# VectorE makes both low parts of an expert's weight block

## The chip, the cores and the metric

The kernel runs on one core of one Trainium2 chip. The metric is the device time of one execution in microseconds (us). A core has TensorE (PE; its weight loads are shown as PEld), VectorE (DVE), ScalarE (ACT), GpSimd (POOL) and SyncE (SP, which here issues most of the DMAs). Each engine runs its own queue in order and waits for the others by semaphores.

## The reference

Attention with pooled keys and values, a token mixer, a channel mixer, and a mixture of eight experts, all in float32:

```python
# attention: 8 batches, 8 heads, 576 tokens, head size 64; keys and values pooled by 8
scores = scale * np.matmul(q, k_p.transpose(0, 1, 3, 2))
attn = softmax(scores);  x = attn @ v_p                  # 8 x 576 x 512
# token mixing, then channel mixing
h = np.maximum(x.transpose(0, 2, 1) @ w_tok1, 0.0) @ w_tok2
u = x + h.transpose(0, 2, 1)
x = u + np.maximum(u @ w_ch1, 0.0) @ w_ch2               # w_ch1 512 x 1536
# experts: each token goes to one of 8
logits = x @ w_gate;  local_gate = sigmoid(x @ w_local)
e = argmax(logits[b, s]) if s == 0 or local_gate[b, s] < 0.5 else prev_e
out[b, s] = p[e] * (np.maximum(x[b, s] @ w1[e], 0.0) @ w2[e])   # w1[e] 512 x 1024, w2[e] 1024 x 512
```

## The kernel before

A matrix in float32 is multiplied as two parts that TensorE takes at full rate: a high part (the value rounded by a cast to float32r) and a low part (the value less its high part). A product is three passes: high by high, low weights by high, high weights by low.

There are three stages. The mixer (attention and token mixing) runs to about 310 us. The channel mixer then works on 18 *slots* of 256 tokens with 6 blocks of 256 hidden features each, to about 936 us. The expert stage works on slots of the tokens of one expert: doubles of 256 tokens, four blocks each, with a single of 128 tokens after every third double in its later part. A step of the pipeline is one block of one slot (`pipeline`): `hidden` (L626; L642 for a single) makes relu(x @ w1 block) in PSUM, ScalarE casts its high part hh (L632) and VectorE its low part hl (L633); `project` (L668), one step later, adds hidden @ w2 block to y. At a slot's last step TensorE transposes the next slot's rows, ScalarE casts their high part xh (L616) and VectorE makes the low part xl (L617). Between the products VectorE computes the router's logits, 18 operations named junk for each 256 tokens of the channel stage (L697), and the tables of the experts' slots.

The weights come in blocks of w1[:, 256 features] and w2[256 features, :], 1 MB in float32. `load_expert` has SyncE load a block into one of four staging buffers st (L579, L583). `split_block` (L589) makes its four parts in a ring of six buffers w: two casts by ScalarE (L593, L595) and two subtractions, the low part of w1 (L594) and that of w2 (L596). With `aside`, for the first two blocks, which are split during the mixer, all four are GpSimd's.

The order on each engine is the order in which this code is written. In a step: the hidden's matmuls, the gathers of coming slots' rows (first step of a slot), the transposes (last step), some of the queued routing work (`drain`), the projects of the step before, and then `stage_to` and `split_to`: the load of the block eight ahead of the one just projected and the split of the block six ahead, whose ring buffer has become free. A cast therefore stands on ScalarE before the next step's hh, and a subtraction on VectorE before the next step's hl.

GpSimd has other work in the same queue: the scatter of each token's entry into the list of its expert (L791, four for each 512 tokens, each waiting for the one before to land), the gather of a slot's rows (L950) and the scatter of its output (L977).

Of the kernel before, what the change touches and what calls it, by code (L numbers as in the profile page):

```python
# [10 lines left out]
F32 = mybir.dt.float32  # L11
# [15 lines left out]
DCH = 1536  # L27
E, FE = 8, 1024

# Attention: 128-row chunks of a batch's (head, pooled key) rows, and the heads that each one meets.  # L30
NCH = 5
CH_ROWS = [128, 128, 128, 128, 64]
CH_HEAD0 = [0, 1, 3, 5, 6]
CH_NH = [2, 3, 3, 3, 2]
NT = 5

# Matrix blocks of 256 hidden features: w1[:, block] and w2[block, :] side by side.
FC = 256
NCC = DCH // FC
NCE = FE // FC  # L40
RING = 6

# Routed tokens: an expert's entries lie in a region of RS entries; DUM is where empty ones lie.
SLOT = 256
NSLOT = NTOK // SLOT
NGROUP = NSLOT // 2
# [5 lines left out]
FIRST_SINGLE = 7  # L52
EVERY = 3
NLATE = NDBL + NSGL
# The slots in the order in which they run: singles between the doubles, and those that may be empty last.
MAYBE = NSLOT + NSTATIC


# [5 lines left out]
RS = NTOK + SLOT  # L64
DUM = E * RS
LR = DUM + SLOT
# The greatest float32 z for which 1 / (1 + exp(-z)) rounds to 0.5 or more lies above this.
GATE = -1.5 * 2.0**-23


# [35 lines left out]


class PoolStack:
    """Tile pools at one end of the memories, released last first."""

    def __init__(self, tc, side):
        self.tc, self.side, self.pools = tc, side, []
# [9 lines left out]


class Slot:
    """A run of up to 256 tokens with the tiles that they are in."""


class Rounding:
    """float64 (as int64 words) rounded to float32, in steps that other work can lie between."""

    def __init__(self, nc, pool, ebias, src):
        self.nc, self.src = nc, src
# [41 lines left out]


def mixer_phase(nc, tc, q, k, v, w_tok1, w_tok2, w_ch1, w_ch2, const, stage, ebias, wc, u, spread):
    """Attention and token mixing: rows of u; and the channel weights in float32."""
    ident, mask = const("ident"), const("mask")
    late, early = PoolStack(tc, "right"), PoolStack(tc, "left")
    wp = late.pool("tokw", 1)  # L180
# [51 lines left out]
    rounding = {}  # L232

    def tok_piece(i):
        """Rounding of the i-th piece of the token weights, and its split."""
        src, h, l = tok_parts[i]
        r = Rounding(nc, cvp, ebias, src)
        r.fields()
        r.scale_here()
        r.size()  # L240
        f = r.sign()
        nc.scalar.copy(h, f)
        nc.gpsimd.tensor_sub(l, f, h.bitcast(F32))
        if i == NT - 1:
            nc.scalar.copy(t1h[64:, i], f)

    def piece(c, part):
        """Part of the rounding of the c-th piece of the channel weights."""
        if not 0 <= c < 4 * NCC:
            return  # L250
        if part == "fields":
            rounding[c] = Rounding(nc, cvp, ebias, ch_st[c // 2][:, c % 2 * 512:c % 2 * 512 + 512])
            rounding[c].fields()
        elif part == "scale":
            rounding[c].scale()
        elif part == "size":
            rounding[c].size()
        else:
            o = c // 2 % 2 * 1024 + c % 2 * 512
            nc.sync.dma_start(out=wc[c // 4, :, o:o + 512], in_=rounding.pop(c).sign())  # L260
# [160 lines left out]
    def mix1(b, t):  # L421
        n = rows(t)
        if t == 0:
            bps[b] = [psb.tile([128, 512], F32, tag=f"b1{m}", name=f"b1{m}") for m in range(2)]
        ps = bps[b]
        xh, xl = xh_t.pop((b, t)), xl_t.pop((b, t))
        for m in range(2):
            ms = slice(m * 128, m * 128 + 128)
            h, l = t1h[:, t, ms], t1l[:n, t, ms]
            # Half a tile of tokens has its two parts one above the other.  # L430
            passes = ((h, xh), (l, xh), (h, xl)) if n == 128 else ((h, xh), (l, xh[:n]))
            for i, (w, x) in enumerate(passes):
                nc.tensor.matmul(
                    ps[m], w, x, start=t == 0 and i == 0, stop=t == NT - 1 and i == len(passes) - 1
                )
# [37 lines left out]
    for c in range(NCH):  # L473
        k_sums(0, c)
    k_blocks(0)
    # The pieces of the channel weights that the steps round: none in those that end a batch's first product.
    pieces = {}
    for n in range(8, NS):
        if n % NT != 1:
# [62 lines left out]


def tail_phase(nc, tc, const, stage, wring_a, wc, w1, w2, w_gl, ctok, cempty, u, x2d, lst, out):
    """Channel mixing, routing and experts, 256 tokens at a time: the part that runs early, and the rest."""
    P = Slot()

    ident, before, rev, region = (const(n) for n in ("ident", "before", "rev", "region"))
# [14 lines left out]
        for r in range(EARLY_GROUPS * 2 * SLOT, NTOK + 128, 128):  # L563
            nc.sync.dma_start(out=x2d[r:r + 128], in_=zero)

# [1 line left out]
    def ring_tile(pos):  # L567
        p = wring_a if pos < 2 else P.ring_b if pos < 4 else P.ring_c
        return p.tile([128, 4, 1024], F32R, tag=f"w{pos}", name=f"w{pos}")
# [17 lines left out]
        return st  # L587

    def split_block(st, pos, aside=False):  # L589
        """A block's parts; aside: by the one engine that has little else to do."""  # L590
        w = ring_tile(pos)
        copy = nc.gpsimd.tensor_copy if aside else nc.scalar.copy
        copy(w[:, 0], st[:, :1024])  # L593
        (nc.gpsimd if aside else nc.vector).tensor_sub(w[:, 1], st[:, :1024], w[:, 0].bitcast(F32))  # L594
        copy(w[:, 2], st[:, 1024:])  # L595
        nc.gpsimd.tensor_sub(w[:, 3], st[:, 1024:], w[:, 2].bitcast(F32))  # L596
        k1 = lambda i: w[:, i].rearrange("p (k f) -> p k f", f=FC)
        k2 = lambda i: w[:, i].rearrange("p (s d) -> p s d", d=DM)
        return k1(0), k1(1), k2(2), k2(3)

# [1 line left out]

    def transpose_rows(sl):
        n = sl.nt * 128
# [12 lines left out]
            nc.vector.tensor_sub(sl.xl[:, ks, :n], ps[:, :, :n], sl.xh[:, ks, :n].bitcast(F32))  # L617

    def hidden(sl, w):
        """relu(x @ w1 block), features on the partitions, in two float32r parts."""  # L620
        w1h, w1l, _, _ = w
        ps = P.psh.tile([128, 2, SLOT], F32, tag="h", name="h")
        passes = [(a, x, k) for a, x in ((w1h, sl.xh), (w1l, sl.xh), (w1h, sl.xl)) for k in range(4)]
        for s in range(2):
            for i, (a, x, k) in enumerate(passes):
                nc.tensor.matmul(  # L626
                    ps[:, s], a[:, k, s * 128:s * 128 + 128], x[:, k],
                    start=i == 0, stop=i == len(passes) - 1,
                )
        hh = P.hT.tile([128, 2, SLOT], F32R, tag="hh", name="hh")  # L630
        hl = P.hT.tile([128, 2, SLOT], F32R, tag="hl", name="hl")
        nc.scalar.activation(hh, ps, AF.Relu)  # L632
        nc.vector.scalar_tensor_tensor(hl, ps, 0.0, hh.bitcast(F32), op0=ALU.max, op1=ALU.subtract)  # L633
        return hh, hl

    def hidden_rows(sl, w):
        """relu(x @ w1 block), tokens on the partitions."""
        w1h, w1l, _, _ = w
        ps = P.psh.tile([128, 2, SLOT], F32, tag="h", name="h")
        passes = [(a, x, k) for a, x in ((w1h, sl.xh), (w1l, sl.xh), (w1h, sl.xl)) for k in range(4)]  # L640
        for i, (a, x, k) in enumerate(passes):
            nc.tensor.matmul(  # L642
                ps[:, 0], x[:, k, :128], a[:, k], start=i == 0, stop=i == len(passes) - 1
            )
        h = P.hT.tile([128, FC], F32, tag="hrow", name="hrow")
        nc.scalar.activation(h, ps[:, 0], AF.Relu)
        return h
# [22 lines left out]
                    start=j == 0 and i == 0, stop=j == sl.nb - 1 and i == len(passes) - 1,  # L670
                )

# [1 line left out]
    queue = deque()  # L674

    def drain(budget):
# [5 lines left out]
            fn()  # L682
            budget -= cost

# [1 line left out]
    state = {"carry": None, "base": None}  # L686
    logit_t = {}

# [113 lines left out]
        queue.append((0.0, sums))  # L802
        queue.append((2.0, place))

# [1 line left out]
    one_row = lambda shape, name: P.route1.tile([1, *shape], F32, name=name)  # L806

    def running(x, name):
# [2 lines left out]
        return y  # L811

    def lookup(cum, first, idx, n, name):
        """For each of n indices: its expert under the running sums, and first[expert]."""
        ge = one_row([n, E], name + "g")
        nc.vector.tensor_tensor(
            ge, cum.rearrange("p (o e) -> p o e", o=1).to_broadcast([1, n, E]),
# [13 lines left out]
        return ex, at  # L831

    def shifted(x, add, shift, name):
        """floor((x + add) / 2 ** shift)"""
        i = P.route1.tile([1, E], I32, name=name + "i")
        nc.vector.tensor_scalar(i, x, float(add), None, op0=ALU.add)
        nc.vector.tensor_scalar(i, i, shift, None, op0=ALU.logical_shift_right)
        y = one_row([E], name)
        nc.vector.tensor_copy(y, i)
        return y  # L840
# [76 lines left out]
        nc.vector.tensor_scalar(ap, ap, float(DUM), None, op0=ALU.add)  # L917
        tables["late"] = table(ep, ap, NLATE, "ltab")

# [1 line left out]
    slots = []  # L921
    for i in range(NSLOT):
        s = Slot()
# [55 lines left out]
                in_=o[:, t], in_offset=None,  # L979
            )  # L980

# [1 line left out]
    blocks = [("c", j) for j in range(NCC)]  # L983
    for s in slots[NSLOT:]:
        s.block = len(blocks)
# [28 lines left out]
    tokid = const("tok")  # L1014

    def ahead(n):
        """Between the steps of the mixer: the first weight blocks."""
        if n == B * NT - 6:
            stage_to(2)
        elif n in (B * NT - 4, B * NT - 2):  # L1020
            split_to(nsplit[0] + 1, aside=True)
            stage_to(nsplit[0] + 2)

    def pipeline(slots, nrows, begin=None):
        # A project follows its hidden by one step, or two where the hidden block is turned first.
        steps = [(s, j) for s in slots for j in range(s.nb)]
        turn, ready = None, []
        for n, (s, j) in enumerate(steps):
# [154 lines left out]
```

## Time and profile before

| what | value |
|---|---|
| time, three runs | 1473.81, 1474.2, 1477.3 us; median 1474.2 |
| profiled execution, span from first to last instruction | 1476.5 us (no other time is listed for it) |
| busy: PE, PEld | 1405.3 (95%), 1241.5 us (84%) |
| busy: DVE, ACT, POOL | 964.6 (65%), 541.9 (37%), 550.7 us (37%) |
| mean granted clock of TensorE | 0.983 |

A line of a timeline tells when an instruction began, how long it took, its engine and line, the tiles it writes and reads, and in brackets how long its engine was idle before it and what ended that. A wait is read by its right side: "PE h L626 <- DVE hl L633" is TensorE idle before a matmul of L626 until VectorE's hl was there. [...]

### The profile page before, as it was taken

How to read it: one execution, taken by the hardware profiler on the slowest of the kernel's cores; microseconds unless marked ns; L12 is line 12 of the kernel's file. 1: busy time of each engine (PE TensorE's matmuls, PEld its weight loads, DVE VectorE, ACT ScalarE, POOL GpSimd, SP SyncE). 2: the span in 40 equal slices, each digit the busy share in tenths (PEclk: the TensorE clock that was granted, in tenths of full speed). 3: DMA queues.
4: the chain of work that ended last, by engine and by line, in shares of the span. 5: the costliest groups of instructions: out<-in, count | busy, mean ns of one | idle time of the engine just before them, and what ended most of it. 6: DMA issues, size and time to landing. Idle time of an engine off the chain costs nothing. (4 is left out here: it accounts for less than half of the span.)

```text
span 1476.5 us, 23732 instructions
## 1 busy us (share of the span) xinstructions
PE 1405.3 (95%) x8724; PEld 1241.5 (84%) x8724; DVE 964.6 (65%) x1880; ACT 541.9 (37%) x1357; POOL 550.7 (37%) x521
## 2 busy tenths in 40 slices
PE   5899999999999999999999999999879899898997
PEld 4677787789999999999999999889769798787986
DVE  6899888854565565656565756886484656666552
ACT  4677777641111111111111112443434454444551
POOL 4787665330010101010000001654665665656652
PEclk9999999999999999999999999999999999999999
DMA  9567776563010111111211113653775757567550
GB/s 265 143 211 221 234 220 196 175 219 109 29 30 29 30 29 30 29 30 30 49 15 52 30 44 115 196 172 133 249 254 175 261 182 249 200 217 256 200 205 24
DMA packets 161530, 204.40 MB, mean 138 GB/s; under 512 B 59568, under 2 KB 104752, under 8 KB 160496
## 3 DMA queue, kind: packets, MB, share of 16 engines
q1 hardware_dynamic: 153856, 181.81, 39.8%
q0 software_dynamic: 7552, 21.02, 3.9%
q8 instruction: 71, 1.16, 0.4%
q14 instruction: 51, 0.42, 0.1%
HBM read 164.68 MB, written 38.36 MB: 138 GB/s over the span
## 5 line engine op out<-in xcount | busy, mean ns | idle before, releaser
L668 PE MATMUL y<-w,hh 128*128 128x512 f32 x1504 | 414.9, 398 | 7.0 <-ACT hh L632 7.0
L626 PE MATMUL h<-xh,w 128*128 128x256 f32 x2880 | 408.3, 285 | 13.7 <-DVE hl L633 13.7
L626 PEld LDWEIGHTS h<-xh,w 128*128 128x128 f32 x2880 | 386.8, 193 | 29.7 <-DVE hl L633 15.3
L632 ACT ACTIVATE hh<-h 128x512 fp32r<-128x512 f32 x180 | 107.6, 598 | 584.4 <-PE h L626 406.9
L668 PEld LDWEIGHTS y<-w,hh 128*128 128x128 f32 x1504 | 271.6, 190 | 55.2 <-ACT hh L632 7.5
L633 DVE SCALAR_TENSOR_TENSOR hl<-h,hh 128x512 fp32r<-128x512 f32 x180 | 124.0, 689 | 276.3 <-ACT hh L632 276.1
L596 POOL TENSOR_TENSOR w<-st,w 128x1024 fp32r<-128x1024 f32 x94 | 234.6, 2514 | 107.4 <-ACT w L595 102.1
L594 DVE TENSOR_TENSOR w<-st,w 128x1024 fp32r<-128x1024 f32 x92 | 191.4, 2081 | 104.6 <-ACT w L593 103.9
L626 PE MATMUL h<-xl,w 128*128 128x256 f32 x1440 | 236.1, 286 | 11.8 <-DVE xl L617 11.4
L697 DVE SCALAR_TENSOR_TENSOR junk<-x,gate 128x512 f32<-128x512 f32 x324 | 234.3, 723 | 9.2
L668 PE MATMUL y<-w,hl 128*128 128x512 f32 x752 | 233.8, 392 | 2.3 <-DVE hl L633 2.3
L791 POOL DMA_INDIRECT entries<-ent,posi x36 | 40.5, 1124 | 516.6 <-DVE posi L789 349.1
L626 PEld LDWEIGHTS h<-xl,w 128*128 128x128 f32 x1440 | 201.1, 194 | 14.0 <-DVE xl L617 13.8
L668 PEld LDWEIGHTS y<-w,hl 128*128 128x128 f32 x752 | 141.9, 189 | 34.2 <-DVE hl L633 2.7
L593 ACT CAST w<-st 128x1024 fp32r<-128x1024 f32 x92 | 96.4, 1048 | 172.5 <-PE y L668 81.5
L364 ACT ACTIVATE e<-qk,mx 128x72 f32<-128x72 f32 (+1 forms) x320 | 97.1, 327 | 13.3 <-DVE sm L375 12.9
L595 ACT CAST w<-st 128x1024 fp32r<-128x1024 f32 x92 | 96.0, 1044 | 2.9 <-DMA st<-in_w_dram 2.9
L977 POOL DMA_INDIRECT out_dram<-x,entry x40 | 48.8, 1221 | 113.5 <-ACT w L593 27.0
L398 PE MATMUL pv<-vblk,aT 128*128 128x192 f32 (+5 forms) x400 | 73.8, 323 | 4.0 <-ACT aT L389 2.0
L398 PEld LDWEIGHTS pv<-vblk,aT 128*128 128x128 f32 (+3 forms) x400 | 58.0, 180 | 21.8 <-issue 10.3
L950 POOL DMA_INDIRECT rows<-x_rows,entry x40 | 45.6, 1141 | 79.7 <-DVE x L959 52.6
L364 ACT ACTIVATION_READ_ACCUMULATOR e<-qk,mx 128x1 f32 (+1 forms) x320 | 68.7, 215 | 0.0
(195 smaller groups left out, 1451.1 us busy)
## 6 DMA issues: line engine op xcount, KB each, us to landing
st<-in_w_dram SPq DMA_DIRECT2D x176, 512.0 KB
chs<-in_w_ch_dram SPq DMA_DIRECT2D x12, 1024.0 KB
rows<-u_rows SPq DMA_DIRECT2D x18, 512.0 KB
x_rows<-x SPq DMA_DIRECT2D x18, 512.0 KB
qin<-in_q_dram SPq DMA_DIRECT2D x32, 256.0 KB
kin<-in_k_dram SPq DMA_DIRECT2D x32, 256.0 KB
vin<-in_v_dram SPq DMA_DIRECT2D x32, 256.0 KB
u_rows<-ut SPq DMA_DIRECT2D x32, 256.0 KB
```

Source lines behind the costliest of these rows:

```text
L364: nc.scalar.activation(e[:n, h], ps[:n, h // 4, h % 4 * SP:h % 4 * SP + SP], AF.Exp, scale=1.0 / 64.0, bias=mx[:n, h:h + 1], accum_out=sm[ ...
L398: nc.tensor.matmul(ps[:n, h0 * D:(h0 + nh) * D], aT[:r, c, :n], vb[b % 2][:r, c, :nh].rearrange("p h d -> p (h d)"), start=c == 0, stop=c ...
L593: copy(w[:, 0], st[:, :1024])
L594: (nc.gpsimd if aside else nc.vector).tensor_sub(w[:, 1], st[:, :1024], w[:, 0].bitcast(F32))
L595: copy(w[:, 2], st[:, 1024:])
L596: nc.gpsimd.tensor_sub(w[:, 3], st[:, 1024:], w[:, 2].bitcast(F32))
L626: nc.tensor.matmul(ps[:, s], a[:, k, s * 128:s * 128 + 128], x[:, k], start=i == 0, stop=i == len(passes) - 1,)
L632: nc.scalar.activation(hh, ps, AF.Relu)
L633: nc.vector.scalar_tensor_tensor(hl, ps, 0.0, hh.bitcast(F32), op0=ALU.max, op1=ALU.subtract)
L668: nc.tensor.matmul(sl.y[t], x[:, s, ts], b[:, s], start=j == 0 and i == 0, stop=j == sl.nb - 1 and i == len(passes) - 1,)
L697: nc.vector.scalar_tensor_tensor(junk, sl.x2[:, t], 1.0, P.gate[:, e], op0=ALU.mult, op1=ALU.mult, accum_out=lt[:, 2 * a + t, e:e + 1],)
L977: nc.gpsimd.indirect_dma_start(out=out, out_offset=bass.IndirectOffsetOnAxis(s.ent[:, t, 0:1], 0), in_=o[:, t], in_offset=None,)
```

## The change

In `split_block` the engine that subtracts is chosen once and makes both low parts: VectorE, or GpSimd in a block that is split aside. Before, the low part of w2 was GpSimd's in every block. The casts and the order of the code are as they were. The rest of the diff takes out comments and docstrings; lines below `split_block` have numbers greater by one.

```diff
     def split_block(st, pos, aside=False):
         w = ring_tile(pos)
         copy = nc.gpsimd.tensor_copy if aside else nc.scalar.copy
-        copy(w[:, 0], st[:, :1024])
-        (nc.gpsimd if aside else nc.vector).tensor_sub(w[:, 1], st[:, :1024], w[:, 0].bitcast(F32))
-        copy(w[:, 2], st[:, 1024:])
-        nc.gpsimd.tensor_sub(w[:, 3], st[:, 1024:], w[:, 2].bitcast(F32))
+        sub = (nc.gpsimd if aside else nc.vector).tensor_sub
+        for i in range(2):
+            half = st[:, i * 1024:i * 1024 + 1024]
+            copy(w[:, 2 * i], half)
+            sub(w[:, 2 * i + 1], half, w[:, 2 * i].bitcast(F32))
```

VectorE's queue where the channel stage passes into the experts' (w_10045 and w_10114 are ring buffers of experts' blocks, x_9812 holds rows of the last but one channel slot). Before:

```order
L697 SCALAR_TENSOR_TENSOR junk,logit<-x_9812,gate 128x512 x4
L594 TENSOR_TENSOR w_10045<-st,w_10045 128x1024
L633 SCALAR_TENSOR_TENSOR hl<-h,hh 128x512
L617 TENSOR_TENSOR xl<-x_10081,xh 128x512
L617 TENSOR_TENSOR xl<-x_10088,xh 128x512
L697 SCALAR_TENSOR_TENSOR junk,logit<-x_9812,gate 128x512 x2
L594 TENSOR_TENSOR w_10114<-st,w_10114 128x1024
```

and after:

```order
L698 SCALAR_TENSOR_TENSOR junk,logit<-x_9812,gate 128x512 x4
L597 TENSOR_TENSOR w_10045<-st,w_10045 128x1024 x2
L634 SCALAR_TENSOR_TENSOR hl<-h,hh 128x512
L618 TENSOR_TENSOR xl<-x_10081,xh 128x512
L618 TENSOR_TENSOR xl<-x_10088,xh 128x512
L698 SCALAR_TENSOR_TENSOR junk,logit<-x_9812,gate 128x512 x2
L597 TENSOR_TENSOR w_10114<-st,w_10114 128x1024 x2
```

Each subtraction has become two, ahead of the next hl; nothing else has moved.

GpSimd's queue in the same stretch, before:

```order
L791 DMA entries<-ent,posi 39168x2 x4
L596 TENSOR_TENSOR w_9868<-st,w_9868 128x1024
L596 TENSOR_TENSOR w_9922<-st,w_9922 128x1024
L596 TENSOR_TENSOR w_9988<-st,w_9988 128x1024
L596 TENSOR_TENSOR w_10045<-st,w_10045 128x1024
L596 TENSOR_TENSOR w_10114<-st,w_10114 128x1024
L950 DMA rows<-x_rows,entry 128x512 x4
```

and after:

```order
L792 DMA entries<-ent,posi 39168x2 x28
L951 DMA rows<-x_rows,entry 128x512 x2
L792 DMA entries<-ent,posi 39168x2 x4
L951 DMA rows<-x_rows,entry 128x512 x6
L978 DMA out_dram<-x_10461,entry 4736x512 x2
```

The subtractions between the scatters and the gathers are gone; the DMAs stand in the same order.

VectorE's queue before the first channel slot (x_3957 and x_3964 are its transposed rows, w_3950 the third channel block), before:

```order
L443 SCALAR_TENSOR_TENSOR hl<-b_3722,hh 128x512
L594 TENSOR_TENSOR w_3950<-st,w_3950 128x1024
L617 TENSOR_TENSOR xl<-x_3957,xh 128x512
L617 TENSOR_TENSOR xl<-x_3964,xh 128x512
L455 TENSOR_TENSOR ut<-b_3973,x 128x512
```

and after:

```order
L443 SCALAR_TENSOR_TENSOR hl<-b_3722,hh 128x512
L597 TENSOR_TENSOR w_3950<-st,w_3950 128x1024 x2
L618 TENSOR_TENSOR xl<-x_3957,xh 128x512
L618 TENSOR_TENSOR xl<-x_3964,xh 128x512
L455 TENSOR_TENSOR ut<-b_3973,x 128x512
```

Here the added subtraction has come ahead of xl.

## Rows read from the trace of the kernel before

**Rows 1.** Waits of PE, 860 us to the end: us in total, times, longest.
```profile
PE h L626 <- DVE hl L633: 13.7, 3, 5.6
PE h L626 <- DVE xl L617: 11.4, 4, 6.0
PE y L668 <- ACT hh L632: 7.0, 2, 6.2
...
PE y L668 <- DVE hl L633: 2.3, 1, 2.3
```

**Rows 2.** Timeline, 1080 to 1120 us: start, us, what [idle before].
```profile
1090.17 11.03 DVE L594 TENSOR_TENSOR w<-st,w 128x1024 fp32r<-128x1024 f32 x1 [2.55 <-ACT w L593]
...
1090.73 9.38 POOL L596 TENSOR_TENSOR w<-st,w 128x1024 fp32r<-128x1024 f32 x4
...
1101.12 0.68 DVE L633 SCALAR_TENSOR_TENSOR hl<-h,hh 128x512 fp32r<-128x512 f32 x1
...
1102.46 1.39 PE L626 MATMUL h<-xl,w 128*128 128x256 f32 x4 [6.03 <-DVE xl L617]
```

**Rows 3.** Lines L594 and L596: count, ns min/median/max; group, busy us, mean ns.
```profile
L594 DVE TENSOR_TENSOR w<-st,w x92: 1205/1226/11033, 307.5 to 1442.0; 128x1024 fp32r<-128x1024 f32 x92
...
L594 POOL TENSOR_TENSOR w<-st,w x2: 2380/2547/2714, 269.2 to 276.9; 128x1024 fp32r<-128x1024 f32 x2
...
L596 POOL TENSOR_TENSOR w<-st,w x94: 2329/2412/3422, 273.0 to 1443.1; 128x1024 fp32r<-128x1024 f32 x94
...
L594 DVE TENSOR_TENSOR w<-st,w 128x1024 fp32r<-128x1024 f32 x92 | 191.4, 2081 | 104.6 <-ACT w L593 103.9 <-issue 0.6
```

**Rows 4.** Windows: start:end, us, then busy us (instructions) PE PEld DVE ACT POOL, PEclk, DMA, GB/s.
```profile
940.00:950.00 10.00, 9.39 (x54) 8.75 (x55) 7.26 (x11) 2.64 (x4) 7.00 (x6) 0.83 0.37 107
...
1100.00:1110.00 10.00, 7.54 (x31) 6.77 (x32) 5.73 (x8) 0.70 (x2) 1.60 (x3) 0.66 0.74 254
...
1350.00:1370.00 20.00, 16.25 (x94) 14.81 (x94) 10.85 (x8) 7.47 (x10) 11.50 (x6) 0.83 0.73 250
```

**Rows 5.** Timeline, 1016 to 1062 us, the chain behind one wait.
```profile
1028.53 0.96 POOL L791 DMA_INDIRECT entries<-ent,posi  x1 [3.18 <-DMA entries<-ent,posi]
...
1029.52 7.04 POOL L596 TENSOR_TENSOR w<-st,w 128x1024 fp32r<-128x1024 f32 x3
...
1031.95 0.37 SPq L579 DMA_DIRECT2D st<-in_w_dram  x1
...
1037.42 1.04 ACT L593 CAST w<-st 128x1024 fp32r<-128x1024 f32 x1 [14.29 <-DMA st<-in_w_dram]
...
1040.84 2.08 PE L668 MATMUL y<-w,hh 128*128 128x512 f32 x4 [6.23 <-ACT hh L632]
```

**Rows 6.** Timeline of DVE, 895 to 1060 us, and a window of the same stretch.
```profile
911.08 0.69 DVE L633 SCALAR_TENSOR_TENSOR hl<-h,hh 128x512 fp32r<-128x512 f32 x1 [2.50 <-ACT hh L632]
...
914.50 1.22 DVE L594 TENSOR_TENSOR w<-st,w 128x1024 fp32r<-128x1024 f32 x1
916.70 0.69 DVE L633 SCALAR_TENSOR_TENSOR hl<-h,hh 128x512 fp32r<-128x512 f32 x1 [0.98 <-ACT hh L632]
...
960.54 3.42 DVE L594 TENSOR_TENSOR w<-st,w 128x1024 fp32r<-128x1024 f32 x1
...
967.14 2.79 DVE L697 SCALAR_TENSOR_TENSOR junk<-x,gate 128x512 f32<-128x512 f32 x1
...
950.00:980.00 30.00, 30.00 (x194) 27.26 (x193) 28.29 (x52) 11.91 (x15) 13.55 (x8) 1.00 0.66 219
```

**Rows 7.** Timeline, 1100 to 1120 us: an hl and the project that reads it.
```profile
1113.36 0.69 DVE L633 SCALAR_TENSOR_TENSOR hl<-h,hh 128x512 fp32r<-128x512 f32 x1 [1.16 <-ACT hh L632]
...
1119.08 0.62 PE L668 MATMUL y<-w,hl 128*128 128x512 f32 x2
```

**Rows 8.** Timeline, 296 to 345 us: the first slot's xl.
```profile
308.97 1.29 DVE L617 TENSOR_TENSOR xl<-x,xh 128x512 fp32r<-128x512 f32 x2 [0.20 <-ACT xh L616]
...
310.55 0.64 PE L626 MATMUL h<-xl,w 128*128 128x256 f32 x4
```

More of the change, by code (lines that the diff above doesn't have):

```diff
@@ L124 @@
 class Slot:
+    pass
 class Rounding:
```

## The prediction

> **What bounds the kernel now.** I read the span and the PE waits first, then the lines, then the timeline around the longest waits. TensorE is busy nearly without a break from the first slot on, so the span is the sum of its matmuls and of whatever makes it wait or run slowly. In the expert stage it stands still four ways [rows 1]: 13.7 us for hl (3 times), 11.4 us for xl (4 times), 7.0 us for hh (twice) and 2.3 us for hl in a project (once), 34.4 us in ten waits. [...] Time lost is one minus the clock, times the stretch: 10 x 0.17 + 2 x 10 x 0.34 + 3 x 20 x 0.17 = 18.7 us.
>
> What causes the waits is seen in one place [rows 2]. At 1090.17 VectorE begins a subtraction of a block (L594) and at 1090.73 GpSimd begins four of its own (L596) back to back, 9.38 us; VectorE's takes 11.03 us and ends 1.1 us after GpSimd's last. Behind it on VectorE stand hl (1101.12) and the next slot's xl, and TensorE waits 6.03 us for xl. The subtraction itself needs 1.226 us (median of 92), yet the longest is 11.033 and GpSimd's median is 2.412 [rows 3]. The other waits for VectorE have a long subtraction or a held logit operation, as in [rows 6], in front of them in the same way.
>
> [...]
>
> One wait has another road [rows 5]. GpSimd issues the scatters of list entries (L791), one per landing (the last at 1028.53, after 3.18 us of waiting), and only then its subtractions, three in a row. SyncE's next load needs the staging buffer that the first of them frees and goes out at 1031.95; ScalarE's cast waits 14.29 us for it, hh stands behind the cast, and TensorE waits 6.23 us. That is GpSimd again, by way of a buffer.
>
> **The change part by part.** *Removed from GpSimd:* the low part of w2 of 92 blocks, 2.41 us each [rows 3]. GpSimd isn't waited for directly at the end, so its own time is worth nothing; what counts is that nothing stands in its queue that can hold VectorE, and that it no longer frees a staging buffer late. Both roads to the waits go: 34.4 + 18.7 = 53.1 us. Idle and low clock overlap a little inside the stretches of [rows 4] (a clock that falls while TensorE still waits costs nothing), so I take 52. Scatters and gathers stay on GpSimd; they come earlier.
>
> The two blocks that are split ahead, during the mixer, stay on GpSimd altogether (its two low parts of w1 are the L594 rows of POOL [rows 3]): no gain or loss there.
>
> *Added to VectorE:* 92 subtractions of the same shape as L594, so 92 x 1.226 = 113 us of work. It also loses what L594 has over its median: mean 2081 against 1226 ns [rows 3], 92 x 0.855 = 79 us, so its sum grows by only some 34 us. What matters is the fullest stretch. While the last logits are computed a step of VectorE is: hl and four logit operations, 911.08 to 914.50 = 3.42 us, then the subtraction [rows 6]; with two it is 3.42 + 2 x 1.226 = 5.87 us, against 5.62 us from one hl to the next (911.08 to 916.70), which is TensorE's pace. Eight steps have four logit operations, so VectorE falls back by 0.25 us in each, 2.0 us at most. Taken another way: from 950 to 980 VectorE is busy 28.29 of 30 us [rows 6]; take off what the two held instructions there lost (3.42 - 1.23 and 2.79 - 0.69, 4.3 us), add 5.3 steps of 1.226 = 6.5 us: 30.5 of 30. Full, about half a microsecond over. What hides it is the lead of hl: one made at 1113.36 is done at 1114.05, and the project that reads it does so at 1119.08, the row of y<-hl [rows 7]: 5.0 us. So 2 us of lag cost TensorE nothing there. For xl, which a new slot's hidden reads early, the lead is shorter, but in the program xl stands ahead of the subtractions of its step and only inherits the lag of earlier ones. After the logits are done a step needs 0.69 + 2.45 us plus a share of xl and of the scaling of the output, far under 5.62. I charge 0.7 us for the whole (bounds 0, and 5 if the lag runs past the lead once and the clock falls with it).
>
> The second subtraction also stands ahead of xl at one place, the very first slot: there xl was made from 308.97 and is read at 310.55 [rows 8]. With 1.23 us more in front, the first of its two halves is ready at 308.97 + 1.23 + 0.65 = 310.85, 0.3 us late. Cost 0.3 us, once.
>
> *Moved:* a staging buffer is now freed by VectorE. SyncE's loads wait for the latest of two readers as before, and the second subtraction follows the cast at once, where GpSimd's came 2.4 us long or behind a queue. No DMA is added and none changes its place in SyncE's queue. But SyncE is in order, and the list entries of a coming slot must wait until the last four scatters (L791) have landed: these still take about 4 us each (1028.53 is 3.18 + 0.96 after the one before [rows 5]), 16 us together, and the loads behind that entry wait with them. So the wait of 6.23 us could come back in part, now because of the entry. GpSimd reaches the scatters sooner, and the loads run two steps (11 us) ahead of their casts. Bounds: 0, and the whole wait with its clock, 6.23 + 3.4 = 9.6 us. I take 1.0, near the lower end, since the loads ahead of the entry no longer wait for GpSimd.
>
> *ScalarE* has the same casts in the same order; a cast waits for the old block's last matmul, as now, and one wait for GpSimd goes.
>
> Sum: -52 + 0.7 + 0.3 + 1.0 = -50.0 us. The profiled execution has a span of 1476.5 us: 1426.5. That span lies 2.3 us above the median of the runs, 1474.2, and inside their range, so the forecast against the median is 1424, with 1 us for what can't be seen: 1425 us.
>
> **The rivals.**
> *The waits come back half* (0.13). VectorE's lag meets an xl, or SyncE's entry holds the loads. For it: VectorE is full in 950 to 980, and SyncE's order. Against it: the leads of 5.0 and 11 us. Price: one stall of the old kind by SyncE, 9.6, and one by VectorE of 5 and its clock of 3.4, about 18 us in all: 1425 + 18 = 1443.
>
> *The subtraction is slow of its own and GpSimd is not the cause; VectorE becomes the bound* (0.04). Then each costs its mean of 2.08 us wherever it stands, the waits stay, and steps with four logit operations need 3.42 + 4.16 = 7.58 us against 5.62: eight of them lose 15.7 us, less the lead of 5: slower by about 11, 1485. It decides from a cost of a subtraction at which eight steps use up the lead: 8 x (3.42 + 2s - 5.62) = 5.0, s = 1.41 us. Against it: the median of 1.226, the jumps in steps of GpSimd's 2.4 us, and the very next instruction beginning on time after a short one.
> [...]
>
> *The change doesn't do what it says* (0.03): GpSimd still holds VectorE by the gathers and scatters that stay, and the same waits return with them: 1474. Against it: of the waits of [rows 1] none stands behind a scatter alone; one takes about 1 us, where the subtractions come three and four in a row.
>
> **How the numbers follow.** The forecast has 0.80, with its own range of 1419 to 1432 (the 53.1 taken whole and no new cost, and the new costs near their middle). The range for 8 in 10 takes in most of the half-way case: 1419 to 1440. A change of 0.3% (4.4 us) is about the least that a measurement of this kernel can tell. Faster: forecast and half-way case, 0.93. Same: 0.03. Slower: 0.04.
>
> **What would show it.** In the profile after: no subtraction of VectorE much over 1.3 us, hl and xl gone from what TensorE waits for, the clock at 1.00 between 930 and the end, TensorE's steps at 5.62 us throughout, POOL busy about 220 us less, DVE some 30 us more. If VectorE's subtractions stay long with no GpSimd arithmetic beside them, or if TensorE waits for hh behind a cast that waits for its load for several microseconds, the reasoning was wrong there.

## The result, and the profile after

The changed kernel takes 1426.55 us (median of 4 runs, 1425.59 to 1426.84) against 1474.01 us of the kernel before (4 runs, 1469.24 to 1477.3): a ratio of 0.9663 by the comparison of the runs, 95% interval 0.9635 to 0.9691 (the two medians alone give 0.968). The forecast was 1425, range 1419 to 1440. The profiled execution has a span of 1425.1 us and took 1426.84.

From the page of the changed kernel, the span and the busy time of each engine:

```profile
span 1425.1 us, 23643 instructions
...
PE 1389.2 (97%) x8724; PEld 1228.9 (86%) x8724; DVE 977.2 (69%) x1972; ACT 542.0 (38%) x1357; POOL 311.7 (22%) x429
```

GpSimd is busy 239 us less, VectorE only 12.6 us more, though it makes 92 more subtractions. TensorE's busy time has fallen by 16 us with the same matmuls. (On float32r parts its matmuls of 512 columns begin 0.23 us apart, at 107.08, 107.31 and 107.54 in the trace of before: 0.45 ns a column. The scores, on float32 tiles, take two matmuls of 144 columns for each product, eight in the 0.98 us from 107.77 to 108.75: 1.7 ns a column.) The windows of the expert stage (columns as in [rows 4]; PEclk is the granted clock of TensorE, 1.00 its full speed) show in one row each where the gain lies. Before:

```profile
936.00:1476.00 540.00, 492.57 (x3082) 444.72 (x3081) 324.73 (x374) 238.27 (x315) 306.26 (x167) 0.96 0.59 200
```

and after:

```profile
936.00:1425.00 489.00, 477.47 (x3086) 432.96 (x3084) 331.07 (x453) 238.39 (x315) 87.80 (x82) 0.99 0.64 218
```

The stage is 51.0 us shorter, practically the whole difference of the spans (51.4). TensorE's idle time in it falls from 540 - 492.57 = 47.4 to 489 - 477.47 = 11.5 us, 35.9 us less; the other 15.1 us are the same matmuls running at a higher granted clock (0.96 before, 0.99 after).

From 930 to 1370 us, in four stretches of which two are shown, and in the fullest stretch of [rows 6], the clock is at 1.00 throughout. It falls (to 0.82) only in the last 15 us, 1410 to 1425, in which TensorE is busy for 6.48:

```profile
930.00:1040.00 110.00, 109.86 (x716) 99.85 (x715) 95.20 (x195) 53.49 (x67) 24.21 (x21) 1.00 0.62 206
1040.00:1150.00 110.00, 109.29 (x708) 99.18 (x707) 70.47 (x79) 54.94 (x73) 20.91 (x21) 1.00 0.74 251
...
950.00:980.00 30.00, 30.00 (x198) 27.46 (x198) 27.89 (x56) 14.36 (x19) 4.49 (x4) 1.00 0.68 229
```

Of the waits of [rows 1] none is left; from 860 us to 1440 the list of TensorE's waits has a single line (total, times, longest). It isn't new: the kernel before has it too (hrow L646, 3.0 us in 4 waits, longest 0.8), which [rows 1] leave out:

```profile
PE h L643 <- ACT hrow L647: 2.9, 4, 0.7
```

The subtractions (now L597; count, ns min/median/max, as in [rows 3]):

```profile
L597 DVE TENSOR_TENSOR w<-st,w x184: 1204/1220/1228, 307.9 to 1393.0; 128x1024 fp32r<-128x1024 f32 x184
...
L597 POOL TENSOR_TENSOR w<-st,w x4: 2371/2406/2706, 269.6 to 280.7; 128x1024 fp32r<-128x1024 f32 x4
```

All 184 of VectorE take their median to within 2%; the longest is 1.228 us, where it was 11.033.

### The profile page after: what moved, and what is told of

The parts are those of the page before. It is cut to its first block, busy times and chain, and to the rows that moved or that the text cites. A ratio compares the mean times of both kernels' runs of the same rounds, so it can differ in the third digit from the quotient of the medians.

```text
span 1425.1 us, 23643 instructions
## 1 busy us (share of the span) xinstructions
PE 1389.2 (97%) x8724; PEld 1228.9 (86%) x8724; DVE 977.2 (69%) x1972; ACT 542.0 (38%) x1357; POOL 311.7 (22%) x429
## 5 line engine op out<-in xcount | busy, mean ns | idle before, releaser
L627 PE MATMUL h<-xh,w 128*128 128x256 f32 x2880 | 401.9, 282 | 0.0
L627 PEld LDWEIGHTS h<-xh,w 128*128 128x128 f32 x2880 | 380.6, 190 | 15.3 <-DVE hl L634 0.9
L597 DVE TENSOR_TENSOR w<-st,w 128x1024 fp32r<-128x1024 f32 x184 | 217.1, 1221 | 111.0 <-ACT w L596 111.0
L596 ACT CAST w<-st 128x1024 fp32r<-128x1024 f32 x184 | 183.9, 1047 | 159.6 <-PE y L669 146.8
L627 PE MATMUL h<-xl,w 128*128 128x256 f32 x1440 | 232.2, 283 | 0.2
L698 DVE SCALAR_TENSOR_TENSOR junk<-x,gate 128x512 f32<-128x512 f32 x324 | 223.7, 691 | 9.2
L627 PEld LDWEIGHTS h<-xl,w 128*128 128x128 f32 x1440 | 197.6, 190 | 1.6 <-DVE xl L618 1.5
L978 POOL DMA_INDIRECT out_dram<-x,entry x40 | 43.0, 1075 | 212.1 <-DVE x L977 101.5
L345 PEld LDWEIGHTS qk<-kblk,qT 128*128 128x128 f32 (+1 forms) x320 | 43.9, 187 | 17.0 <-ACT e L364 8.2
L345 PE MATMUL qk<-kblk,qT 128*128 128x144 f32 (+1 forms) x320 | 50.3, 302 | 7.8 <-ACT e L364 5.1
```

The lines of the kernel that those rows point to most:

```text
L345: nc.tensor.matmul(ps[:n, i // 2, (i % 2) * 2 * SP:(i % 2 + 1) * 2 * SP], qT[:, i, :n], kb[b % 2][:, i].rearrange("p j s -> p (j s)"), sta ...
L596: copy(w[:, 2 * i], half)
L597: sub(w[:, 2 * i + 1], half, w[:, 2 * i].bitcast(F32))
L627: nc.tensor.matmul(ps[:, s], a[:, k, s * 128:s * 128 + 128], x[:, k], start=i == 0, stop=i == len(passes) - 1,)
L698: nc.vector.scalar_tensor_tensor(junk, sl.x2[:, t], 1.0, P.gate[:, e], op0=ALU.mult, op1=ALU.mult, accum_out=lt[:, 2 * a + t, e:e + 1],)
L978: nc.gpsimd.indirect_dma_start(out=out, out_offset=bass.IndirectOffsetOnAxis(s.ent[:, t, 0:1], 0), in_=o[:, t], in_offset=None,)
```

## The experiments

Each is an edit of the changed kernel unless it says "of the kernel before". Where one adds an instruction, its result is used by nothing (`tick` is one column, `idle` a private tile of 128 x 1024, `st` and `w` are as in the kernel). Two theories stood against each other: GpSimd's *arithmetic on SBUF operands* shuts VectorE out, or GpSimd's *place in the chain* (it frees staging buffers late, issues DMAs late) does it. The kernel before took 1472.6 to 1477.6 us (medians) in the comparisons that follow, the changed kernel 1426.2 to 1426.6 in two; differences to the changed kernel across comparisons are good to a few us.

**A subtraction of GpSimd on a private tile (e1_idle_sub).** It waits for the block's cast, as the old one did, but frees no staging buffer. If the arithmetic alone holds VectorE, most of the loss comes back, 1455 to 1480 us.

```diff
+        if not aside:
+            nc.gpsimd.tensor_copy(tick, w[:, 2, :1].bitcast(F32))
+            nc.gpsimd.tensor_sub(idle, idle, idle)
```

> The changed kernel, and beside it, in each block that is not split aside, GpSimd first copies one column of w2's high part (so that it waits for the cast, as its subtraction did) and then subtracts a private 128x1024 tile from itself. Nothing uses the result and no staging buffer waits for GpSimd. [...] Rival (GpSimd was late as a producer and as the last user of a staging buffer): no subtraction over 1.3 us, 1424 to 1432 us.

Measured 1457.64 us (1453.05 to 1460.23), ratio to the kernel before 0.9881 [0.9855, 0.9906]. The two lines:

```profile
L597 DVE TENSOR_TENSOR w<-st,w x184: 1203/1220/3662, 307.5 to 1419.2; 128x1024 fp32r<-128x1024 f32 x184
...
L600 POOL TENSOR_TENSOR idle<-idle x92: 1883/1887/2962, 308.8 to 1422.2; 128x1024 f32<-128x1024 f32 x92
```

and TensorE's waits:

```profile
PE h L630 <- DVE xl L621: 9.1, 4, 4.0
PE h L656 <- DVE hl L660: 4.6, 3, 1.5
```

The waits for xl and hl are back, though the subtraction shares no data and no buffer with any other engine. The longest, 4.0 us for xl at 944.68, stands behind three logit operations in a row that took 2.40 us each instead of 0.69. So GpSimd's subtraction alone holds VectorE (VectorE's longest takes 3.66 us, the median 1.22), and the edit costs 31 of the 47 us. Not all of the 31 need be holds: the copy reads a ring buffer, and ScalarE's casts wait for GpSimd to have come past it (21.2 us in 9 waits; 11.8 in 6 in the kernel before); the next experiment shows that a full GpSimd queue costs of itself. A subtraction now loses at most 3.66 - 1.22 = 2.4 us, little more than one GpSimd subtraction of 1.89 us takes, never four of them: between two of these stands a copy of one column.

**GpSimd only writing (e2_idle_memset).** The same place, three memsets of the tile (2.9 us a block).

```diff
+            nc.gpsimd.tensor_copy(tick, w[:, 2, :1].bitcast(F32))
+            for _ in range(3):
+                nc.gpsimd.memset(idle, 0.0)
```

> As the run before this one, but instead of the subtraction GpSimd fills the private tile three times, which only writes SBUF (about 3 us a block, more than the 2.4 us of a subtraction). If what holds VectorE is GpSimd reading SBUF: no long subtraction, 1424 to 1432 us. If any busy GpSimd instruction on SBUF holds it: as with the subtraction, 1455 us or more.

Measured 1443.75 us (1440.67 to 1446.42), ratio 0.9776 [0.9745, 0.9807]: neither number. No subtraction is held:

```profile
L597 DVE TENSOR_TENSOR w<-st,w x184: 1201/1220/1303, 308.1 to 1411.2; 128x1024 fp32r<-128x1024 f32 x184
```

The 17 us come by another way, which the timeline shows at one place:

```profile
946.77 2.97 POOL L601 MEMSET idle<- 128x1024 f32 x3
...
954.08 1.97 POOL L955 DMA_INDIRECT rows<-x_rows,entry  x1 [0.30 <-issue]
...
958.51 0.34 SPq L965 DMA_DIRECT2D x_rows<-x  x1
959.12 0.37 SPq L579 DMA_DIRECT2D st<-in_w_dram  x1
...
965.11 1.04 ACT L596 CAST w<-st 128x1024 fp32r<-128x1024 f32 x1 [10.07 <-DMA st<-in_w_dram]
...
968.49 1.92 PE L631 MATMUL h<-xh,w 128*128 128x256 f32 x7 [4.84 <-ACT xh L621]
```

The gathers (L955) stand behind the memsets. SyncE's store of x rows must wait for them; SyncE's own waits from 940 to 970 us have the row

```profile
SPq L965 <- DMA rows<-x_rows,entry: 19.6, 2, 17.7
```

and the load of a block stands behind that store. ScalarE's cast waits 10.07 us for the load, and TensorE 4.84 us for the xh behind that cast. The holds went as the first theory says (the memsets, which only write, held no subtraction: 1.303 us at most); that a busy GpSimd queue costs so much by DMAs it issues, I had not counted.

**The staging buffer freed by GpSimd (e3_late_buffer).** One column read by GpSimd is enough to make SyncE wait for it.

```diff
+        if not aside:
+            nc.gpsimd.tensor_copy(tick, st[:, 2047:])
```

> The changed kernel, and GpSimd copies one column of each staging buffer, in the place in its queue where its subtraction stood: a buffer is again freed only when GpSimd has come past its scatters and gathers, but GpSimd does next to no arithmetic. Theory: only the one wait by way of SyncE comes back (6.2 us and 3.4 us of low clock, perhaps a second one of the kind), 1430 to 1442 us. Rival (the late buffers were the main cause): most of the 47 us come back, over 1455 us.

Measured 1431.45 us (1430.85 to 1432.29), ratio 0.9696 [0.9673, 0.9719]. SyncE does wait for GpSimd:

```profile
SPq L579 <- POOL tick L599: 133.6, 25, 16.0
```

and it costs 5 us, some 3.5 of them at the list entry (the step that begins at 1031.11 in the changed kernel begins at 1034.61); no wait of TensorE comes back into the list. The road over the buffer is real and, by this, small. It may be more than these 5 us: the copy waits for the load alone, not for the cast, and in the kernel before SyncE waited 233.0 us in 51 waits for GpSimd's subtractions.

**Half of the old share (e4_every_other).** GpSimd makes the low part of w2 in odd blocks only.

```diff
-        sub = (nc.gpsimd if aside else nc.vector).tensor_sub
...
-            sub(w[:, 2 * i + 1], half, w[:, 2 * i].bitcast(F32))
+            own = aside or (i == 1 and pos % 2)
+            (nc.gpsimd if own else nc.vector).tensor_sub(w[:, 2 * i + 1], half, w[:, 2 * i].bitcast(F32))
```

> GpSimd makes w2's low part in every other block, VectorE in the rest. Theory: GpSimd has at most two subtractions in a row, a hold of VectorE ends within about 6 us and mostly inside the lead of 5 us that hl has, so most of the gain stays: 1426 to 1440 us. If the loss goes with the number of GpSimd's subtractions: half of 47 us, 1450 us.

Measured 1440.59 us (1438.69 to 1446.79), ratio 0.9765 [0.9726, 0.9805]. Half of the subtractions bring back 14 of 47 us, less than half, 0.6 us over the first range and far from 1450:

```profile
L597 DVE TENSOR_TENSOR w<-st,w x138: 1203/1224/5844, 309.8 to 1406.9; 128x1024 fp32r<-128x1024 f32 x138
```

The longest hold is 5.84 - 1.22 = 4.6 us, up to two instructions of GpSimd: it has fewer to put in a row.

**A third subtraction on VectorE (e5_third_sub).** How much room is left there?

```diff
+        if not aside:
+            nc.vector.tensor_sub(idle, idle, idle)
```

> The changed kernel with a third subtraction of 1.2 us on VectorE in each block, of a private tile from itself; GpSimd as in the changed kernel. It asks how much room VectorE had. By the terms of the prediction a step with four logit operations then needs 3.42 + 3 x 1.22 = 7.1 us against 5.62: a lag of 1.5 us a step, 5 us after four of them, and xl, whose lead is about 2 us, comes late in the passage from the channel to the experts' stage, two or three waits of 2 to 5 us with low clock behind them; in the other steps 0.69 + 3.66 + 0.7 = 5.1 us fit. 1433 to 1448 us, no subtraction over 1.3 us. If VectorE had been the bound already with two: 92 x 1.2 = 110 us more, 1537 us.

Measured 1463.39 us (1462.43 to 1464.27), ratio 0.9929 [0.9912, 0.9946]: 37 us more than the changed kernel, over the range. A step with four logit operations in VectorE's timeline:

```profile
922.77 0.68 DVE L636 SCALAR_TENSOR_TENSOR hl<-h,hh 128x512 fp32r<-128x512 f32 x1
...
926.18 2.36 DVE L597 TENSOR_TENSOR w<-st,w 128x1024 fp32r<-128x1024 f32 x2
928.46 1.22 DVE L599 TENSOR_TENSOR idle<-idle 128x1024 f32<-128x1024 f32 x1
929.59 0.69 DVE L636 SCALAR_TENSOR_TENSOR hl<-h,hh 128x512 fp32r<-128x512 f32 x1
```

From hl to hl it takes 929.59 - 922.77 = 6.82 us where TensorE needs 5.62, and here VectorE is the bound. That part (some 20 us from 936 to 1050) I had in the sum. Left out were the four slots of 128 tokens. From the first hidden of such a slot to that of the next slot TensorE takes 18.5 us in the changed kernel (1125.06 to 1143.56) and 20.9 us here (1146.92 to 1167.86); VectorE, with 12 subtractions there in place of 8, is busy for 19.0 of the 22 us from 1146 to 1168. With a late step that follows, each of the four places loses 2.5 to 4 us, some 15 in all. With two subtractions a block VectorE has room, but less than one more.

**The kernel before in pieces of 256 columns (e6_four_pieces).** If one whole instruction holds VectorE, shorter ones should hold it less: under 1445 us if VectorE gets in behind any piece, 1474 to 1490 us if a row of pieces keeps it out as the whole instructions did.

```diff
-        nc.gpsimd.tensor_sub(w[:, 3], st[:, 1024:], w[:, 2].bitcast(F32))
+        for c in range(4):
+            a, z = c * 256, c * 256 + 256
+            nc.gpsimd.tensor_sub(w[:, 3, a:z], st[:, 1024 + a:1024 + z], w[:, 2, a:z].bitcast(F32))
```

> The kernel before, but GpSimd makes its low part in four instructions of 256 columns in place of one of 1024. [...]

Measured 1462.66 us (1459.04 to 1469.8), ratio 0.9918 [0.9898, 0.9938], between the two. VectorE's and GpSimd's lines:

```profile
L594 DVE TENSOR_TENSOR w<-st,w x92: 1203/1226/3997, 307.0 to 1434.4; 128x1024 fp32r<-128x1024 f32 x92
...
L598 POOL TENSOR_TENSOR w<-st,w x376: 712/732/1786, 273.3 to 1441.2; 128x256 fp32r<-128x256 f32 x188
```

The subtractions lose much less: 25 of the 92 took over 1.35 us, but most of these under 1.9, and only two about 4. The longest hold fell on a logit operation, which no line of a subtraction shows (timeline, 920 to 940 us):

```profile
924.62 11.77 DVE L699 SCALAR_TENSOR_TENSOR junk<-x,gate 128x512 f32<-128x512 f32 x1
924.70 11.13 POOL L598 TENSOR_TENSOR w<-st,w 128x256 fp32r<-128x256 f32 x16
```

Sixteen pieces in a row kept it out for 11.77 - 0.69 = 11.1 us, longer than anything in the kernel before, and TensorE waits 4.1 us for the hl behind it. In another row of sixteen (from 1095.50) VectorE's subtractions at 1104.10 and 1106.95 took 1.24 and 1.47 us and the piece beside each 1.7 us in place of 0.73: there VectorE got in between two pieces. So pieces that follow one another at once may keep VectorE out and may not; which, these runs don't settle. GpSimd now needs 4 x 0.73 = 2.9 us a block, SyncE waits 300.0 us for it (233.0 before), and ScalarE for the loads and TensorE behind it:

```profile
PE h L644 <- ACT hrow L648: 22.3, 4, 7.5
```

Part of the cost has moved from VectorE to the buffers. The experiment doesn't price the holds.

**The kernel before with a gap behind GpSimd's subtraction (e7_gap).** The same arithmetic, but a copy of one column of its result stands behind each, so that no two follow each other at once. If VectorE gets in there, 1436 to 1455 us; if not, 1474 us or more.

```diff
         nc.gpsimd.tensor_sub(w[:, 3], st[:, 1024:], w[:, 2].bitcast(F32))
+        nc.gpsimd.tensor_copy(tick, w[:, 3, 1023:].bitcast(F32))
```

> The kernel before, but behind each of its subtractions GpSimd copies one column of the result, which has to wait for the subtraction to end. GpSimd's work stays and grows a little; only its instructions no longer follow each other at once. [...]

Measured 1447.45 us (1446.26 to 1450.61), ratio 0.982 [0.9804, 0.9837]: with more work on GpSimd, 25 us are won (the kernel before took 1472.62 in this comparison). The longest subtraction falls from 11.033 to 3.849:

```profile
L594 DVE TENSOR_TENSOR w<-st,w x92: 1203/1226/3849, 307.3 to 1414.9; 128x1024 fp32r<-128x1024 f32 x92
```

and the timeline shows the two engines taking turns, near the place of [rows 2]:

```profile
1099.80 2.40 POOL L596 TENSOR_TENSOR w<-st,w 128x1024 fp32r<-128x1024 f32 x1
1102.25 0.19 POOL L597 COPY tick<-w 128x1 f32<-128x1 f32 x1
1102.39 2.40 POOL L596 TENSOR_TENSOR w<-st,w 128x1024 fp32r<-128x1024 f32 x1
1104.24 1.64 DVE L594 TENSOR_TENSOR w<-st,w 128x1024 fp32r<-128x1024 f32 x1 [0.37 <-ACT w L593]
1104.86 1.06 POOL L597 COPY tick<-w 128x1 f32<-128x1 f32 x1
1105.88 2.39 POOL L596 TENSOR_TENSOR w<-st,w 128x1024 fp32r<-128x1024 f32 x1
```

VectorE's subtraction loses the 0.4 us until GpSimd's is done; GpSimd's next work then waits for VectorE (its copy takes 1.06 us instead of 0.19) and starts as that ends. So a gap was enough here to let VectorE in. Of what is left of the loss, 21 us, the two longest waits of TensorE show two roads: 5.95 us for xl at 945.90, behind three logit operations of 2.3 to 2.9 us and a subtraction of 3.35, each held once, and 4.29 us for hh at 1044.90, behind a load for which ScalarE's cast waited 12.81 us.

**No part for GpSimd at all (e8_none_aside).** The two blocks split ahead go to ScalarE and VectorE too.

```diff
-            split_to(nsplit[0] + 1, aside=True)
+            split_to(nsplit[0] + 1)
```

> The changed kernel with the first two blocks split by ScalarE and VectorE as well, so that GpSimd takes no part at all. Theory: it takes away the one long VectorE instruction left (2.6 us at 281 us, beside GpSimd's subtraction) and adds four casts and four subtractions to two engines that are 70 to 85% busy there: within 3 us of the changed kernel, 1423 to 1430 us.

Measured 1423.96 us (1422.8 to 1424.46), ratio 0.9661 [0.9645, 0.9677]. Two waits that the changed kernel has between 250 and 330 us

```profile
PE b L453 <- DVE x L405: 1.5, 1, 1.5
PE pv L398 <- ACT qT L337: 0.5, 1, 0.5
```

aren't in its list. To see whether 2 us are real, both were run again on one chip, five rounds each.

> The changed kernel again, to stand on the same chip as the run that follows: 1424 to 1429 us.

> The changed kernel with the first two blocks also split by ScalarE and VectorE, on the same chip as the run before this one. If its lead of 2.6 us (0.2%) in the first comparison is real, 1 to 4 us below it in every run; if it was the chip, within 1 us of it.

The changed kernel took 1426.22 us (1425.69 to 1426.79; ratio 0.9658 [0.9635, 0.9681]), the one without aside 1424.07 (1423.05 to 1425.26; ratio 0.9642 [0.9619, 0.9665]). The runs of the two don't overlap: 2.15 us, 0.15%, and the fastest of the versions here.

## Why the prediction was right, step by step

*Both roads to the waits go: -52.* Right, and of the right size: 35.9 us of idle time (34.4 forecast) and 15.1 us of slower matmuls (18.7), 51.0 together. The 1.1 us that the list entry costs (below) are already taken off in it, so 52.1 against 52. The cause was named right: e1 brings the holds (3.66 us at most) and the waits back by arithmetic on a tile of its own, and e2's memsets, which read no operand in SBUF, hold no subtraction (1.303 us at most). What the holds alone are worth of the 47 us isn't shown: the edits that put work back on GpSimd bring back the delay in its queue with it (e2: 17 us without a hold). The 18.7 us are one minus PEclk, summed over six stretches of the trace of before: the three of [rows 4] and 1030 to 1050 us (0.83), 1170 to 1180 (0.66) and 1260 to 1280 (0.83). Of these 90 us TensorE is busy for 68.15. No run shows a time lost of 18.7 us; in its place the busy times of the stage gave 15.1.

The prediction took from [rows 2] that four of GpSimd's subtractions in a row keep VectorE out. Four in a row do not always hold VectorE so long, even in the kernel before (timeline, 926 to 940 us):

```profile
926.68 10.99 POOL L596 TENSOR_TENSOR w<-st,w 128x1024 fp32r<-128x1024 f32 x4
...
932.64 2.75 DVE L697 SCALAR_TENSOR_TENSOR junk<-x,gate 128x512 f32<-128x512 f32 x1
```

Three logit operations in this row took 2.78, 2.75 and 2.77 us (0.69 is the median): each lost no more than one subtraction, not the whole row. Where GpSimd has a gap (e7), no hold was much longer than one instruction; where the next follows at once, VectorE sometimes got in and sometimes stood out for the whole row [rows 2]. A loss of about one GpSimd instruction fits e7 and e1 (a subtraction of at most 3.85 and 3.66 us) and these three operations. It doesn't fit [rows 2] and the 11.77 us of e6, where VectorE's instruction began first by the recorded starts (1090.17 before 1090.73, 924.62 before 924.70) and stood out for a whole row. What decides between the two was not seen.

*VectorE's lag while the logits last: 0.7.* It cost nothing, but the lag was larger than the sum had it. The first steps with four logit operations in VectorE's timeline after:

```profile
915.34 2.35 DVE L597 TENSOR_TENSOR w<-st,w 128x1024 fp32r<-128x1024 f32 x2
917.62 0.68 DVE L634 SCALAR_TENSOR_TENSOR hl<-h,hh 128x512 fp32r<-128x512 f32 x1
...
921.03 2.36 DVE L597 TENSOR_TENSOR w<-st,w 128x1024 fp32r<-128x1024 f32 x2
923.30 0.68 DVE L634 SCALAR_TENSOR_TENSOR hl<-h,hh 128x512 fp32r<-128x512 f32 x1
```

From hl to hl 5.68 us, against 5.87 forecast and TensorE's 5.62: two subtractions take 2.36 us, not 2 x 1.226, as the second begins before the first has ended, and hl 0.08 us before the end of the pair. Over three such steps (917.62 to 934.67) VectorE falls 0.2 us behind. In the second group, the fullest stretch, it is otherwise:

```profile
958.36 0.69 DVE L634 SCALAR_TENSOR_TENSOR hl<-h,hh 128x512 fp32r<-128x512 f32 x1
...
979.06 0.68 DVE L634 SCALAR_TENSOR_TENSOR hl<-h,hh 128x512 fp32r<-128x512 f32 x1
...
982.05 0.62 PE L669 MATMUL y<-w,hl 128*128 128x512 f32 x2
```

From hl to hl the three steps take 6.87, 7.00 and 6.83 us. An xl pair (1.2 us), the scaling of an output (1.3) and the router's first table operations, with a wait for ScalarE, stand in them, and the sum of 3.42 + 2 x 1.226 had none of these. The hl of 979.06 comes 7.4 us after its hidden began (971.69), that of 917.62 came 3.8 after (913.84): 3.6 us of lag, against 2.0 "at most". It is done at 979.74 and read at 982.05, so 2.3 us of lead were left, and no wait for VectorE is in the list. That the lag cost nothing was right by the lead of 5.0 us that the prediction gave as the reason; the bound on the lag was too low. e5 measures the other side: a third subtraction makes 6.82 us, and the time goes up by 37 us. The room was there, in the lead, but only for one.

*First slot: 0.3.* It costs a little more. The timeline after:

```profile
307.91 2.36 DVE L597 TENSOR_TENSOR w<-st,w 128x1024 fp32r<-128x1024 f32 x2 [0.25 <-ACT w L596]
...
310.19 1.28 DVE L618 TENSOR_TENSOR xl<-x,xh 128x512 fp32r<-128x512 f32 x2
...
311.52 0.30 PEld L627 LDWEIGHTS h<-xl,w 128*128 128x128 f32 x2 [0.30 <-DVE xl L618]
```

xl begins at 310.19, 1.22 us later than in [rows 8], and the weight load waits 0.30 us for it; the whole first step takes 7.56 us instead of 7.09, so 0.47.

*SyncE held at the list entry: 1.0.* Measured 1.1, at the place and by the road foretold; compare [rows 5]:

```profile
1018.70 0.96 POOL L792 DMA_INDIRECT entries<-ent,posi  x1 [3.51 <-DMA entries<-ent,posi]
...
1022.47 0.37 SPq L947 DMA_DIRECT2D entry<-entries  x1
1023.10 0.37 SPq L579 DMA_DIRECT2D st<-in_w_dram  x1
...
1027.19 1.05 ACT L596 CAST w<-st 128x1024 fp32r<-128x1024 f32 x1 [4.65 <-DMA st<-in_w_dram]
...
1029.99 0.59 ACT L633 ACTIVATE hh<-h 128x512 fp32r<-128x512 f32 x1
...
1031.11 1.45 PE L627 MATMUL h<-xh,w 128*128 128x256 f32 x8
```

The load goes out only behind the entry, which waits for the last scatter; the cast waits 4.65 us instead of 14.29. The steps that begin at 1024.5 and 1031.1 take 6.62 and 6.54 us instead of 6.47 and 5.62. That this is less than the whole old wait is as the leads have it, and e3 agrees: a buffer freed late by GpSimd cost 5 us there, though SyncE waited 25 times for it. TensorE's list has no wait for hh at this place.

*From the span to the median: small, and the wrong way.* The forecast span was 1426.5 and came out as 1425.1; the forecast median was put 1.5 us under the span, and the measured one lies 1.45 us over it. The time of an execution is 1.7 to 2.2 us above its span in all runs that list both, which the prediction left out; and the profiled execution of before, with a span of 1476.5, was one of its slower ones. The spans are 51.4 us apart, the medians 47.5: forecast were 50.0 and 49.2. The span came 1.4 us lower than forecast and the median 3.0 us higher against the span; that these two have opposite signs, so that the median is only 1.6 us off, is luck. The runs of before spread over 1469 to 1481 in the comparisons made, those of the changed kernel over 1425.6 to 1426.8. That the waits of before depend on which engine came first, and so differ from run to run, would explain the spread; only one trace of before is kept, so it isn't shown.

*The rivals.* Waits that come back half (1443): no. VectorE bound (1485): a subtraction costs 1.22 us alone and 1.14 in a pair, under the point of 1.41 (in 89 of the 92 pairs the second subtraction begins 1.13 to 1.14 us after the first). That GpSimd's DMAs hold VectorE (1474): in the expert stage no hold is left (the longest subtraction takes 1.228 us), with every gather and scatter still there.

*What would show it.* Most came as listed. TensorE's steps in the expert stage were at their old pace but for the two at the list entry (6.62 and 6.54 us), and the clock was at 1.00 up to 1410 us. VectorE's busy time grew by 12.6 us, not by 30. Its subtractions grew by 25.7 (191.4 in [rows 3] to 217.1), and 10.6 us went from the logit operations, whose mean fell from 723 to 691 ns: they too had been held, one for 2.8 us [rows 6], and I had left that out.

## What to carry to other kernels

Work that was given to an idle GpSimd was not free here: its subtractions, 2.41 us each and all operands in SBUF, held VectorE's subtractions for up to 11.03 us (the median is 1.226) and its logit operations for up to 2.8 (0.69). Look at the maximum of VectorE's instructions against their median, and at what GpSimd does in the same microseconds. Before moving it, count what the receiving engine has to do in its fullest step, against the pace of the engine that bounds: here one subtraction more fitted (5.68 against 5.62 us, and up to 7.0 where other work fell in the step, covered by a lead of 5 us) and two did not (6.82). Work that held nobody still delayed what stood behind it in GpSimd's queue (17 us in e2). If the work must stay on GpSimd, a short dependent instruction between two long ones was worth 25 of the 47 us.

## What the runs showed of the hardware that I had not expected

- GpSimd instructions with nothing between them can keep VectorE out as one: four subtractions for 11.03 us [rows 2], sixteen short ones for 11.77 (e6). They don't always: in other such rows VectorE got in after one (926.68 in the kernel before, 1104.10 in e6). With a copy of one column between, 3.85 us was the most (e7).
- GpSimd's memsets (0.95 us for 128 x 1024) held no subtraction (1.303 us at most, e2).
- VectorE's hl and xl, which read one operand from PSUM, weren't held even in the kernel before: the 180 hl of 128 x 512 took 668 to 694 ns there, the 80 xl 692 at most. Those with two operands in SBUF were: the subtraction, the logits (up to 2.8 us). So was one with a single operand in SBUF: a mask of the mixer (L149, 128 x 512) takes 2.59 us at 280.84 in the changed kernel, beside GpSimd's subtraction of 280.71 (2.43 us), where the median is 0.54; without that subtraction the longest is 0.73 (e8).
- In pieces of 256 columns GpSimd's 1024 columns cost 2.9 us instead of 2.41; 25 of VectorE's 92 subtractions were still held, most by under 0.7 us (e6).
